# Attention and two expert layers on one core: values product of the float32 tiles turned over, last two experts of the fill on two PSUM banks

## The chip, the cores and the metric

The kernel runs on one core of a Trainium2 chip. The metric is the device time of one execution in microseconds (us). Five engines work side by side, each through its own queue in order: PE (matrix products, with PEld for its weight loads), DVE, ACT, POOL, and SP, which here only issues transfers (DMA).

## The reference, cut to what matters

```
q, k, v: (4, 8, 576, 64)           # batch, heads, tokens, head width
scores = q @ k^T / 8
keep, in each row, the scores >= the 32nd largest; softmax over them
x = attn @ v                        # then laid out as 2304 tokens x 512
h = x @ w_in;  x = (h * cos(h)) @ w_out            # w_in 512x2048, first layer
P = exp(x @ w_gate - max), 8 rounds of row and column scaling   # 2304 x 8
out = sum over e of P[:, e] * (relu(x @ w1[e]) @ w2[e])         # 8 experts, 512x1024x512
```

## The kernel before

A Python planner records every operation with a cost, the buffers that it reads and writes and a priority by engine and class of work, then plays the engines forward and emits the operations in the order in which its own clock would start them. Each engine then runs its queue in that fixed order. An operation may be planned ahead of earlier recorded ones, but never ahead of a recorded one that uses the same buffer: `add` (L120 on) makes a write wait for every operation recorded earlier that reads or writes that buffer.

Nearly all products are made of three float32r products: `mm3` splits both sides into a high and a low part and issues high x high (L372), low x high (L373) and high x low (L374). The first three token tiles (384 tokens) go through plain float32 products instead.

The program in the order in which it is recorded:

- Decode of w_in and w_out (DVE, ACT, POOL), beside it the **first attention**: `attention_tile(0..2)`, three tiles of 128 tokens with 8 heads each. Each head runs `att_tile` with `plain`: scores (L451) to ACT, eight-at-a-time maximum and replace three times on DVE (L459, L464, L465), the masked exponentials with their row sum (L466), the reciprocal (L469), the multiplication of the whole 128x576 tile by it on POOL (L470), five transposes on PE (L475), copies to `at_f` on ACT (L479). Then `attention_tile` itself multiplies by v (L530), which puts a head's 64 output columns on partitions and the tokens on the free side in `ps_t`, and ACT copies this into `x_f` (L534).
- The first layer of those tiles in float32 (`moe1_tile_a` and `moe1_tile_b`, L629 to L661), into `x2fh`, `x2fl`.
- `attention(0, LEAD)`: the rest of batch 0, now with the split products (L447, L448, L501, L503).
- **First block of the fill**: `fill(e, 0, LEAD, two)` for the 8 experts and the first 384 tokens. For each of 8 column groups f of w1 a product into one PSUM bank from a ring (`h_ring`), ReLU and split by ACT and DVE (`gates`, L758, L759), and the product with w2 into `ps_y`.
- `attention(1)`, first layer for 512 tokens (`moe1`, then `keep_parts` into `x2fh`, `x2fl`), `attention(2)`, `attention(3)`.
- **Second block of the fill**: `fill(e, LEAD, 4, ...)` for 8 experts and those 512 tokens. The ring of banks is `two` (`ps_g`, `ps_h`) for e below 6 and `three` (`ps_g`, `ps_s`, `ps_h`) for e = 6 and 7:

```
    two, three = Cycle([ps_g, ps_h]), Cycle([ps_g, ps_s, ps_h])
    ...
    for e in range(NE):
        fill(e, LEAD, 4, two if e < 6 else three)
```

- The first layer of the other 1408 tokens in three parts (`moe1` on the ring `three`), the gating, and then all experts for the last 1408 tokens (`mixed_first`, `plain_first`, `mixed_second`), with which the program ends.

`ps_s` is also where every score product of every attention tile goes (L447, L448, L451), and `ps_t` takes transposes and values products. There are 8 banks in all: `ps_y` (4), `ps_h`, `ps_t`, `ps_s`, `ps_g`.

Of the kernel before, what the change touches and what calls it, by code (L numbers as in the profile page):

```python
# [229 lines left out]
def fused_kernel(tc, kq, vv, w_in, w_out, w_gate, w1, w2, out, B=4):  # L230
# [179 lines left out]
    at_r = ring_of("first", 2, [128, 5, 128], F32, "at_f")  # L410
    xf_r = ring_of("first", 2, [128, 4, 128], F32, "x_f")
# [24 lines left out]
    def att_tile(stats, dests, plain=None):  # L436
# [33 lines left out]
        put("POOL", 724, lambda: G_.tensor_scalar(ex.ap, ex.ap, mc(35), 0.0, op0=ALU.mult, op1=ALU.add), [ex, (m, 35, 36)], [ex])  # L470
        pt = lambda: ps_t.ap.rearrange("p (c t) -> p c t", c=4)
        for c0, c1, p in ((0, 4, 128), (4, 5, 64)):
# [8 lines left out]
            for r0, rn, hd, t0 in dests:  # L481
# [12 lines left out]
                put("DVE", dve_ns(k), lambda hv=hv, sv=sv, lv=lv: V.tensor_tensor(lv(), sv(), hv().bitcast(F32), op=ALU.subtract), [ps_t, hi], [lo])  # L494

# [15 lines left out]
    def attention_tile(t):  # L511

        nonlocal work
        work = "first attention"
        x_f, q = xf_r(), qp_r()
        s0 = t * 128
        dma(lambda: q.ap, lambda: kq[0:H, 0:64, 1, s0 : s0 + 128].rearrange("h d s -> d h s"), 1 << 18, writes=[q], slow=True)
        for pr in range(H // 2):
            k, v = kp_r(), vp_r()
            hs = slice(2 * pr, 2 * pr + 2)  # L520
            dma(lambda k=k, hs=hs: k.ap, lambda hs=hs: kq[hs, 0:64, 0, :].rearrange("h d s -> d h s"), 512 * S, writes=[k], slow=True)
            dma(lambda v=v: v.ap, lambda hs=hs: vv[hs].rearrange("h p c d -> p h c d"), 128 * 2560, writes=[v])
            for j in range(2):
                at_f = at_r()
                att_tile([], [], dict(q=q, k=k, at=at_f, h=2 * pr + j))

                def av(v=v, j=j, at_f=at_f):
                    for c in range(5):
                        p = 64 if c == 4 else 128
                        T_.matmul(ps_t.ap[:64, :128], v.ap[:p, j, c, :], at_f.ap[:p, c, :], start=c == 0, stop=c == 4)  # L530

                put("PE", 1100.0, av, [v, at_f], [ps_t])
                r = slice(64 * j, 64 * j + 64)
                put("ACT", act_ns(128, psum=True), lambda pr=pr, r=r: A_.activation(x_f.ap[r, pr, :], ps_t.ap[:64, :128], AF.Copy), [ps_t], [(x_f, pr, pr + 1)])  # L534
        work = "mlp"
        return x_f
# [477 lines left out]
    for e in range(NE):  # L1014
        fill(e, LEAD, 4, two if e < 6 else three)
# [78 lines left out]
```

## Time and profile before

| | us |
|---|---|
| three runs | 2527.22, 2522.58, 2526.36 (median 2526.36) |
| profiled execution | 2523.42 |
| its span on the core | 2521.6 |
| mean granted TensorE clock | 0.971 of full speed |

The span is the time from the first to the last instruction; the profiled execution's own time is 1.8 us more. Busy time of PE is modelled for pipelined products, so neighbouring matmul rows overlap: the distance of their starts is what a product costs in a row of them. "Rows" of the trace give the start, the duration, engine and line, then output and inputs.

### The profile page before, as it was taken

What the parts mean: (1) busy time and instruction counts of PE and PEld (TensorE: products, weight loads), DVE (VectorE), ACT (ScalarE), POOL (GpSimd) and SP (SyncE); (2) the same over time, 40 slices, a digit from 0 to 9 for tenths busy, and PEclk for the clock granted to TensorE, in tenths of its full rate; (3) what the DMA queues carried; (4) which work ended last, traced back from release to release, by engine and by line L of the source; (5) the groups of instructions that cost most, each with busy time, mean ns of one, the idle gap of its engine ahead of it and who ended that gap; (6) DMA issues with size and microseconds to landing.
All of it is one profiled execution on the core that took longest, in us unless ns stands there. A gap on an engine that the chain in (4) does not pass through costs nothing.

```text
span 2521.6 us, 33547 instructions
## 1 busy us (share of the span) xinstructions
PE 2389.5 (95%) x11089; PEld 1919.8 (76%) x11089; DVE 1981.5 (79%) x3651; ACT 1272.9 (50%) x2438; POOL 1265.6 (50%) x1328
## 2 busy tenths in 40 slices
PE   6888999999889999997799999999999999999999
PEld 3444688888667877776588788788888888888887
DVE  8997599999989999999927778776666665666655
ACT  6785576666578656565346767422222222232221
POOL 6886587777676656565340113533333434444330
PEclk9779999999899999998799999999999999999999
DMA  8765654444322433332043333112222221111101
GB/s 265 228 211 185 201 155 150 137 139 131 99 91 78 120 116 117 109 117 77 26 132 114 106 108 115 48 55 79 71 72 84 84 72 34 34 34 46 38 21 46
DMA packets 159501, 261.37 MB, mean 104 GB/s; under 512 B 15008, under 2 KB 60656, under 8 KB 159328
## 3 DMA queue, kind: packets, MB, share of 16 engines
q1 hardware_dynamic: 159328, 259.24, 33.9%
q8 instruction: 87, 1.43, 0.2%
q14 instruction: 86, 0.70, 0.1%
HBM read 227.31 MB, written 31.87 MB: 103 GB/s over the span
## 4 chain that ended last, share of the span: by engine, by line
PE 56%; DVE 22%; POOL 4%; issue 3%; ACT 3%; DMA 1%; POOLq 0%; ACTq 0%; DVEq 0%
PE y L372 9%; PE y L373 9%; PE y L374 9%; DVE wk L464 6%; DVE m L465 5%; DVE ex L466 3%; PE g L374 2%; PE g L373 2%; PE g L372 2%; DVE atl L494 2%; DVE m L459 2%; POOL wlo L347 1%; PE y L383 1%; PE y L384 1%; PE y L387 1%
## 5 line engine op out<-in xcount | busy, mean ns | idle before, releaser
L347 POOL TENSOR_TENSOR wlo<-raw,whi 128x512 fp32r<-128x512 f32 x336 | 452.7, 1351 | 203.0 <-ACT whi L345 131.9
L465 DVE MAX8 m<-wk 128x8 f32<-128x576 f32 x432 | 318.0, 748 | 1.8
L953 DVE SCALAR_TENSOR_TENSOR acc<-y,P,acc 128x512 f32<-128x512 f32 x308 | 229.2, 748 | 103.4 <-PE y L374 103.0
L345 ACT ACTIVATE whi<-raw 128x512 fp32r<-128x512 f32 x416 | 258.9, 626 | 97.3 <-PE y L374 34.0
L464 DVE MATCH_REPLACE8 wk<-m,wk 128x576 f32<-128x576 f32 x288 | 213.6, 742 | 1.2
L475 PE MATMUL t<-ident,ex 128*128 128x128 f32 (+1 forms) x720 | 143.3, 301 | 55.8 <-DVE atl L494 20.6
L475 PEld LDWEIGHTS t<-ident,ex 128*128 128x128 f32 (+1 forms) x720 | 89.5, 145 | 122.3 <-DVE atl L494 32.4
L372 PE MATMUL y<-whi,gh 128*128 128x512 f32 x448 | 181.6, 405 | 0.0
L372 PE MATMUL y<-gh,xh 128*128 128x512 f32 x450 | 176.0, 391 | 1.0 <-DVE acc L949 1.0
L374 PE MATMUL y<-whi,gl 128*128 128x512 f32 x448 | 176.5, 394 | 0.0
L373 PE MATMUL y<-wlo,gh 128*128 128x512 f32 x448 | 175.9, 393 | 0.0
L373 PE MATMUL y<-gl,xh 128*128 128x512 f32 x450 | 175.5, 390 | 0.0
L374 PE MATMUL y<-gh,xl 128*128 128x512 f32 x450 | 175.4, 390 | 0.0
L457 ACT ACTIVATE sc<-s 128x288 f32<-128x288 f32 x288 | 117.0, 406 | 97.4 <-DVE ex L466 55.6
L466 DVE SCALAR_TENSOR_TENSOR ex<-sc,m,ex 128x576 f32<-128x576 f32 x144 | 149.7, 1039 | 3.6 <-ACT ex L461 1.8
L493 ACT ACTIVATE ath<-t 64x128 fp32r<-64x128 f32 (+3 forms) x272 | 104.5, 396 | 58.9 <-PE t L475 52.2
L470 POOL TENSOR_SCALAR ex<-ex,m 128x576 f32<-128x576 f32 x144 | 111.4, 774 | 38.1 <-DVE m L469 36.0
L461 ACT ACTIVATE ex<-sc,m 128x576 f32<-128x576 f32 x144 | 111.2, 772 | 32.1 <-POOL m L460 31.0
L459 DVE MAX8 m<-sc 128x8 f32<-128x576 f32 x144 | 106.9, 743 | 8.7 <-ACT sc L457 8.6
L464 DVE MATCH_REPLACE8 wk<-m,sc 128x576 f32<-128x576 f32 x144 | 106.7, 741 | 0.0
L468 POOL TENSOR_SCALAR m<-m 128x1 f32<-128x1 f32 x144 | 29.2, 202 | 146.5 <-DVE ex L466 141.3
L372 PEld LDWEIGHTS y<-gh,xh 128*128 128x128 f32 x450 | 84.5, 188 | 19.6 <-DVE acc L949 1.8
(384 smaller groups left out, 7150.5 us busy)
## 6 DMA issues: line engine op xcount, KB each, us to landing
raw<-in_w_dram SPq DMA_DIRECT2D x384, 256.0 KB, 2.6
kq<-in_kq_dram SPq DMA_DIRECT2D x32, 576.0 KB, 4.1
raw<-win_d SPq DMA_DIRECT2D x64, 256.0 KB, 3.0
raw<-wout_d SPq DMA_DIRECT2D x64, 256.0 KB, 2.7
y_d<-st SPq DMA_DIRECT2D x56, 256.0 KB, 3.0
raw<-y_d SPq DMA_DIRECT2D x56, 256.0 KB, 2.6
wp<-win_d SPq DMA_DIRECT2D x24, 512.0 KB, 5.0
wp<-wout_d SPq DMA_DIRECT2D x24, 512.0 KB, 4.4
```

The costliest lines, as they stand in the source:

```text
L345: put("ACT", act_ns(n), lambda: A_.activation(hv(), rv(), AF.Copy), [rb], [hb])
L347: put(e, c, lambda: f.tensor_tensor(lv(), rv(), hv().bitcast(F32), op=ALU.subtract), [rb, hb], [lb])
L372: T_.matmul(o(), ah(), bh(), start=start, stop=False)
L373: T_.matmul(o(), ah(), bl(), start=False, stop=False)
L374: T_.matmul(o(), al(), bh(), start=False, stop=stop)
L457: put("ACT", act_ns(288, psum=True), lambda c=c: A_.activation(sc.ap[:, c], o(), AF.Copy), [ps_s], [(sc, c.start, c.stop)])
L459: put("DVE", 669, lambda: V.max(mc(0, 8), sc.ap), [sc], [(m, 0, 8)])
L464: put("DVE", 669, lambda r=r, src=src: V.match_replace(wk.ap, mc(8 * r, 8), src.ap, LOWEST), [src, (m, 8 * r, 8 * r + 8)], [wk])
L465: put("DVE", 669, lambda r=r: V.max(mc(8 * r + 8, 8), wk.ap), [wk], [(m, 8 * r + 8, 8 * r + 16)])
L466: put("DVE", 729, lambda: V.scalar_tensor_tensor(ex.ap, sc.ap, mc(31), ex.ap, op0=ALU.is_ge, op1=ALU.mult, accum_out=mc(33)), [sc, ex, (m, ...
L475: T_.transpose(pt()[:p, c - c0, :], ex.ap[:, c * 128 : c * 128 + p], ident.ap)
L953: put("DVE", 663, lambda y=y, av=av, pcol=pcol: V.scalar_tensor_tensor(av(), y.ap, pcol(), av(), op0=ALU.mult, op1=ALU.add), [y, P, a], [a])
```

## The change

Two things are changed.

1. In the float32 tiles the POOL multiplication by the reciprocal of the row sum goes. The values product takes the attention weights `at_f` as the stationary side and v as the moving one, so the tokens stand on output partitions and a head fills 64 columns of `ps_g`. ACT evicts these 64 columns into a new tile `x_t` (128 tokens x 512) and multiplies by the reciprocal, one number a partition, in the same instruction. After the eighth head four transposes into `ps_t` and one ACT copy make `x_f` as it was.
2. Experts 6 and 7 of the second block of the fill use the ring of two banks as well.

```
+    xt_r = ring_of("first", 2, [128, 512], F32, "x_t")
...
-        put("POOL", 724, lambda: G_.tensor_scalar(ex.ap, ex.ap, mc(35), 0.0, op0=ALU.mult, op1=ALU.add), [ex, (m, 35, 36)], [ex])
+        if not plain:
+            put("POOL", 724, lambda: G_.tensor_scalar(ex.ap, ex.ap, mc(35), 0.0, op0=ALU.mult, op1=ALU.add), [ex, (m, 35, 36)], [ex])
...
-                        T_.matmul(ps_t.ap[:64, :128], v.ap[:p, j, c, :], at_f.ap[:p, c, :], start=c == 0, stop=c == 4)
-
-                put("PE", 1100.0, av, [v, at_f], [ps_t])
-                r = slice(64 * j, 64 * j + 64)
-                put("ACT", act_ns(128, psum=True), lambda pr=pr, r=r: A_.activation(x_f.ap[r, pr, :], ps_t.ap[:64, :128], AF.Copy), [ps_t], [(x_f, pr, pr + 1)])
+                        T_.matmul(ps_g.ap[:, d], at_f.ap[:p, c, :], v.ap[:p, j, c, :], start=c == 0, stop=c == 4)
+
+                put("PE", 1100.0, av, [v, at_f], [(ps_g, h, h + 1)])
+                put("ACT", act_ns(64, psum=True, ap=True), lambda d=d, rv=rv: A_.activation(x_t.ap[:, d], ps_g.ap[:, d], AF.Copy, scale=rv()), [(ps_g, h, h + 1), rb], [(x_t, h, h + 1)])
+
+        def tr():
+            for c in range(4):
+                T_.transpose(ps_t.ap[:, c * 128 : c * 128 + 128], x_t.ap[:, c * 128 : c * 128 + 128], ident.ap)
+
+        put("PE", 436.0, tr, [x_t, ident], [ps_t])
+        put("ACT", act_ns(512, psum=True), lambda: A_.activation(x_f.ap, ps_t.ap.rearrange("p (c t) -> p c t", c=4), AF.Copy), [ps_t], [(x_f, c, c + 1) for c in range(4)])
...
-        fill(e, LEAD, 4, two if e < 6 else three)
+        fill(e, LEAD, 4, two)
```

The planner makes a new order out of it on every engine. (In the changed kernel the lines after the first edit count a few more: scores L448 and L449, transposes L477, values products L504 and L506.) Three places of PE's queue:

PE before, late in `attention(3)`: the last score products (into `s`), transposes (into `t`), and then the first fill product of the group that takes the bank `s`. There is no fill product in the 82 rows ahead of it.

```order
L448 MATMUL s_107<-kl1_1425,qt1_1380 128x288
L475 MATMUL t_226<-ident_82,ex2_223 64x128
L475 MATMUL t_226<-ident_82,ex0_137 128x128 x4
L447 MATMUL s_107<-kh0_1383,qt0_1372 128x288
L448 MATMUL s_107<-kl0_1388,qt0_1372 128x288
L447 MATMUL s_107<-kh1_1400,qt1_1380 128x288
L448 MATMUL s_107<-kl1_1425,qt1_1380 128x288
L475 MATMUL t_226<-ident_82,ex0_137 64x128
L372 MATMUL s_107<-x2fh_1460,whi2_1681 128x512
L373 MATMUL s_107<-x2fl_1463,whi2_1681 128x512
```

All score products of the kernel stand ahead of the first fill product into `s`.

PE in the change, the same stretch of `attention(3)`: score products for the same 64-token tile (`qt`) and fill products into `h` and `y`.

```order
L374 MATMUL y3_1327<-whi1_1620,gl7_2134 128x512
L448 MATMUL s_107<-kh1_1358,qs1_1374 128x288
L449 MATMUL s_107<-kl1_1366,qs1_1374 128x288
L372 MATMUL h_735<-x2fh_1467,whi2_1625 128x512
L373 MATMUL h_735<-x2fl_1469,whi2_1625 128x512
L374 MATMUL h_735<-x2fh_1467,wlo2_1644 128x512
L372 MATMUL h_735<-x2fh_1467,whi2_1625 128x512
L373 MATMUL h_735<-x2fl_1469,whi2_1625 128x512
L374 MATMUL h_735<-x2fh_1467,wlo2_1644 128x512
L477 MATMUL t_195<-ident_82,ex0_137 128x128 x4
L448 MATMUL s_107<-kh0_1295,qt0_1278 128x288
L449 MATMUL s_107<-kl0_1306,qt0_1278 128x288
```

The fill of the last two experts now runs between the scores. By the last attention product of the kernel PE has issued 477 of the 512 high x high products of the fill's first halves in the order before, and 511 in the change.

PE in the change, the end of attention: the last values product (`vs`), the last fill product into `g` and the products into `y` that follow it. The first layer's next part begins 28 rows behind the last values product; before, it begins 226 rows behind it.

```order
L506 MATMUL t_195<-atl1_1887,vs1_1391 128x320
L504 MATMUL t_195<-ath1_1874,vs1_1391 128x320
L372 MATMUL g_229<-x2fh_1467,whi0_1614 128x512
L373 MATMUL g_229<-x2fl_1469,whi0_1614 128x512
L374 MATMUL g_229<-x2fh_1467,wlo0_1622 128x512
L372 MATMUL y0_654<-whi1_1620,gh6_2052 128x512
```

## Rows read from the trace of the kernel before

**Rows 1.** The page's slices: PE, DVE and granted clock, tenths in 40 slices.
```profile
PE   6888999999889999997799999999999999999999
...
DVE  8997599999989999999927778776666665666655
...
PEclk9779999999899999998799999999999999999999
```

**Rows 2.** Windows: us, busy (count) of PE, PEld, DVE, ACT, POOL, clock, DMA.
```profile
882.00:1008.00 126.00, 123.24 (x617) 99.26 (x617) 123.46 (x267) 76.21 (x165) 75.79 (x97) 1.00 0.38 116
...
1450.00:2521.00 1071.00, 1058.73 (x4886) 896.82 (x4884) 706.34 (x1051) 350.79 (x609) 395.51 (x334) 1.00 0.20 61
```

**Rows 3.** Windows of 20 us around the end of attention, same columns.
```profile
1100.00:1120.00 20.00, 19.64 (x97) 15.11 (x96) 19.84 (x42) 13.68 (x30) 13.03 (x18) 1.00 0.54 173
...
1160.00:1180.00 20.00, 16.87 (x86) 13.01 (x85) 19.59 (x43) 13.75 (x30) 14.39 (x19) 0.98 0.35 99
1180.00:1200.00 20.00, 8.91 (x28) 5.71 (x27) 19.81 (x46) 7.48 (x16) 3.34 (x9) 0.50 0.00 0
1200.00:1220.00 20.00, 9.92 (x41) 7.52 (x41) 19.81 (x47) 7.78 (x19) 4.97 (x11) 0.67 0.04 9
1220.00:1240.00 20.00, 15.03 (x56) 11.34 (x54) 19.74 (x47) 6.65 (x15) 2.37 (x7) 0.57 0.02 5
1240.00:1260.00 20.00, 18.41 (x85) 14.04 (x85) 18.53 (x42) 9.12 (x18) 11.50 (x15) 1.00 0.24 68
```

**Rows 4.** PE's timeline: fill's last and next products, next part's first.
```profile
1173.89 0.39 PE L373 MATMUL g<-x2fl,whi 128*128 128x512 f32 x1
1174.13 0.40 PE L374 MATMUL g<-x2fh,wlo 128*128 128x512 f32 x1
...
1231.76 0.44 PE L448 MATMUL s<-kl,qt 128*128 128x288 f32 x1
...
1232.70 0.79 PE L372 MATMUL s<-x2fh,whi 128*128 128x512 f32 x1
...
1322.17 0.39 PE L372 MATMUL s<-xh,whi 128*128 128x512 f32 x1
```

**Rows 5.** DVE's timeline: a gate's low part, the last masked exponentials.
```profile
1241.57 0.68 DVE L759 SCALAR_TENSOR_TENSOR gl<-s,gh 128x512 fp32r<-128x512 f32 x1
...
1256.67 0.82 DVE L466 SCALAR_TENSOR_TENSOR ex<-sc,m,ex 128x576 f32<-128x576 f32 x1
```

**Rows 6.** Timelines of DVE, POOL, ACT and PE, first attention's end.
```profile
225.38 0.92 DVE L466 SCALAR_TENSOR_TENSOR ex<-sc,m,ex 128x576 f32<-128x576 f32 x1
...
231.61 0.75 POOL L470 TENSOR_SCALAR ex<-ex,m 128x576 f32<-128x576 f32 x1
...
241.01 0.27 ACT L534 ACTIVATE x_f<-t 64x128 f32<-64x128 f32 x1 [2.08 <-PE t L530]
...
242.73 1.88 PE L629 MATMUL y<-wp,x_f 128*128 128x512 f32 x4
...
287.07 0.39 PE L372 MATMUL g<-x2fh,whi 128*128 128x384 f32 x1
```

**Rows 7.** Groups by shape, 0 to 290 us: count, busy us, mean ns, idle before.
```profile
L466 DVE SCALAR_TENSOR_TENSOR ex<-sc,m,ex 128x576 f32<-128x576 f32 x26 | 31.4, 1206 | 0.3
...
L470 POOL TENSOR_SCALAR ex<-ex,m 128x576 f32<-128x576 f32 x26 | 21.3, 818 | 7.9 <-DVE m L469 7.7
...
L479 ACT ACTIVATE at_f<-t 128x512 f32<-128x512 f32 x24 | 14.2, 590 | 7.6 <-PE t L475 7.6
...
L534 ACT ACTIVATE x_f<-t 64x128 f32<-64x128 f32 x24 | 6.4, 268 | 14.4 <-PE t L530 14.0
```

**Rows 8.** Groups of PE, 0 to 290 us, same columns.
```profile
L530 PE MATMUL t<-at_f,vp 128*64 128x128 f32 (+1 forms) x240 | 43.2, 328 | 7.2 <-ACT at_f L479 7.2
...
L475 PE MATMUL t<-ident,ex 128*128 128x128 f32 (+1 forms) x129 | 31.2, 354 | 15.9 <-ACT at_f L479 6.8 <-POOL ex L470 4.5 <-ACT x_f L534 2.2
```

**Rows 9.** Groups by shape of DVE, 1180 to 1240 us, same columns.
```profile
L466 DVE SCALAR_TENSOR_TENSOR ex<-sc,m,ex 128x576 f32<-128x576 f32 x9 | 7.3, 812 | 0.2
```

More of the change, by code (lines that the diff above doesn't have):

```diff
@@ L494, in att_tile @@
                 put("DVE", dve_ns(k), lambda hv=hv, sv=sv, lv=lv: V.tensor_tensor(lv(), sv(), hv().bitcast(F32), op=ALU.subtract), [ps_t, hi], [lo])
+        return (m, 35, 36), lambda: mc(35)
     def att_out(hd, x32, j, n):
@@ L514, in attention_tile @@
         work = "first attention"
-        x_f, q = xf_r(), qp_r()
+        x_f, x_t, q = xf_r(), xt_r(), qp_r()
         s0 = t * 128
@@ L521, in attention_tile, with av @@
             dma(lambda k=k, hs=hs: k.ap, lambda hs=hs: kq[hs, 0:64, 0, :].rearrange("h d s -> d h s"), 512 * S, writes=[k], slow=True)
-            dma(lambda v=v: v.ap, lambda hs=hs: vv[hs].rearrange("h p c d -> p h c d"), 128 * 2560, writes=[v])
+            dma(lambda v=v, hs=hs: v.ap, lambda hs=hs: vv[hs].rearrange("h p c d -> p h c d"), 128 * 2560, writes=[v])
             for j in range(2):
-                at_f = at_r()
-                att_tile([], [], dict(q=q, k=k, at=at_f, h=2 * pr + j))
-                def av(v=v, j=j, at_f=at_f):
+                at_f, h = at_r(), 2 * pr + j
+                rb, rv = att_tile([], [], dict(q=q, k=k, at=at_f, h=h))
+                d = slice(h * 64, h * 64 + 64)
+                def av(v=v, j=j, at_f=at_f, d=d):
                     for c in range(5):
                         p = 64 if c == 4 else 128
-                        T_.matmul(ps_t.ap[:64, :128], v.ap[:p, j, c, :], at_f.ap[:p, c, :], start=c == 0, stop=c == 4)
-                put("PE", 1100.0, av, [v, at_f], [ps_t])
-                r = slice(64 * j, 64 * j + 64)
-                put("ACT", act_ns(128, psum=True), lambda pr=pr, r=r: A_.activation(x_f.ap[r, pr, :], ps_t.ap[:64, :128], AF.Copy), [ps_t], [(x_f, pr, pr + 1)])
+                        T_.matmul(ps_g.ap[:, d], at_f.ap[:p, c, :], v.ap[:p, j, c, :], start=c == 0, stop=c == 4)
[6 more added lines that the diff above has]
+        put("ACT", act_ns(512, psum=True), lambda: A_.activation(x_f.ap, ps_t.ap.rearrange("p (c t) -> p c t", c=4), AF.Copy), [ps_t], [(x_f, c, c + 1) for c in range(4)])
         work = "mlp"
```

## Prediction

> **What bounds the kernel now.** I read the page's slices first. Each slice is 63 us. DVE shows eights and nines up to the twentieth, but for the fourth and fifth, and drops after; PE shows nines from the fifth slice on, except for eights in the eleventh and twelfth and two sevens in the nineteenth and twentieth, 1135 to 1260 us [rows 1]. So there are two halves. While attention runs (to about 1260 us) DVE and PE are both full: 123.5 and 123.2 of 126 us in one window. After 1450 us only PE is: 1059 of 1071 us, with DVE at 706 [rows 2]. What changes the end is therefore time in which PE does not get ahead; the reader should look for stretches where PE is idle or at the lower clock and ask what it waits for.
>
> The largest such stretch is the end of attention. In the windows of 20 us PE falls from 19.6 us busy to 8.9, 9.9 and 15.0, with the granted clock at 0.50, 0.67 and 0.57, so mostly at 1.2 GHz, while DVE stays at 19.7 to 19.8 [rows 3]. PE's timeline says what is missing: no fill product between 1174.1 and 1232.7 us. The next one writes `ps_s` and starts just after the last score product of the kernel (1231.8) [rows 4]. That is the rule of the planner: fill products recorded after all attention may not take `ps_s` before all score products are through. Experts 6 and 7 use that bank; their second halves accumulate in order of f, so the group that waits for it holds the rest. From 1232.7 PE then works off the two experts, alone after attention ends, until the next part starts at 1322.2 [rows 4]. That start is my mark: behind it PE is the bound in both kernels and the queues hold the same work.
>
> **The ring of two banks, what it gives.** Lost time of PE in a window is its idle time plus busy time times (1 - clock), if work at 1.2 GHz takes twice as long (an estimate). From 1160 to 1260 us: 3.5 + 15.5 + 13.4 + 11.4 + 1.6 = 45.4 us; five windows of full running lose 5 x 0.36 = 1.8 us [rows 3]. **-44 us**, if PE has fill work at hand all the time. It has: the order of the change puts the products of experts 6 and 7 between the scores, and 511 of 512 of the counted products are issued by the last attention product, where it was 477. The same mix of attention and fill ran before with PE at 19.64 and DVE at 19.84 of 20 us [rows 3], so the mix itself has a row.
>
> **What is given back.** In the order PE stands further behind attention than before when it gets there: at the 600th of the 720 transposes of attention probabilities it has issued 2348 fill products against 2396. 48 products by 0.23 to 0.24 us from start to start [rows 4] are **+11 us**, which come after that point instead of ahead of it.
>
> DVE gets 8 gates (low parts) ahead of its last masked exponentials that it did later before: 8 x 0.6 to 0.68 us = 5 us [rows 5]. On DVE's own path the end comes at 1256.7 + 5 us and the shift of the start (below, 5 us): 1267; from there the last tile needs transposes, evictions and its values product among the last fill products, some 70 rows of PE, 17 us by 0.23 us each. That is 1284 us, ahead of PE's own path (1322 - 44 + 11 + 5 = 1294), so these gates cost nothing as long as PE is the later one; that cover is 10 us.
>
> **The float32 tiles.** Removed: 24 POOL multiplications of 0.82 us [rows 7]. They sit on the way from the row sum to the transposes. In the middle of the first attention this is hidden, since DVE is full. At its end it is not: the last masked exponentials start at 225.4, the last POOL multiplication runs only at 231.6, behind work of the next attention in POOL's queue, and the last copy into `x_f` is at 241.0 [rows 6], 15 us in all. In the change this chain is five transposes (31.2 / 26 = 1.2 us a head), two copies (0.6 and 0.3), the values product (43.2 / 24 = 1.8 us), the scaled copy (0.3), four transposes (1.0) and a copy (0.6 us) [rows 7, 8]: 5.8 us and some eight hand-overs; I take 7 us, so 8 us sooner.
>
> The values product: 240 records, two a product, 43.2 us in all [rows 8]. With 64 moving columns for 128 and 128 stationary for 64 the trace has no such form. Its bounds are half the time (-21 us of PE) and the longer of the weight loads showing (0.35 us, the transposes' record of 128 columns [rows 8], +5 us). All of it lies beside DVE's full queue; at the end of the chain one head counts, -0.9 to +0.2 us. I take 0. The scaled eviction of 128x64 stands between the 0.27 us of the old copy and the 0.59 us of a copy of 512 columns [rows 7]; nearest is 0.27, and only the last head's shows. Added are 12 transposes and 3 copies of 512 columns, of which one set per tile is in the chain above.
>
> Against that stands the order. Behind the last float32 values product PE now has 50 float32 products of the first layer ahead of the fill, where it had 44: six by 0.86 us (four records, two products, in 1.88 us, less the overlap with the next [rows 6]), +5 us. With 5 us that DVE gains earlier (next part) the fill, which began at 287.1 us [rows 6], begins near 279. But DVE then has 20 rows of attention less behind it (310 rows ahead of its first gate, 330 before). An instruction of DVE takes 0.46 us on the mean of a window [rows 2] and 0.81 us for a pass over 576 columns [rows 9], which most of these are: 9 to 16 us, I take 13. Attention is thus late by 13 - 8 = **+5 us**. Bounds: -5 (the chain gains as above and DVE makes the rows good in a gap) and +13 (no gain at the start).
>
> **A rule weighed.** The masked exponentials, with two inputs from SBUF, take 1.21 us in the first 290 us, where POOL decodes, and 0.81 us from 1180 to 1240, where POOL is nearly idle [rows 7, 9]. So POOL's work stretches DVE's: 26 x 0.39 = 10 us in this group alone. Removing 20 us of POOL's work should return a part of that; I take 5 us, half of this group's, counted above. The Trainium skill, "SBUF — State Buffer", section "Who interferes with whom", says that the two share a port pair as an exclusive lock held for a whole instruction, so that the later one fully blocks; by it the removed work could return up to its whole 20 us, and the sum would be 15 us lower. The rows show stretching of the size of a part, not of all of it; the full size is a rival below.
>
> **Sum.** -44 + 11 + 5 = -28 us on the profiled execution's 2523.4 us (span 2521.6): 2495.4. The profiled execution is 2.9 us under the median of the runs, and within their 2522.6 to 2527.2; I forecast about half of that more: **2497 us** as the median.
>
> **Rivals.**
> - *More comes back.* POOL's removed work returns nearly in full to DVE's stage, 15 us more: 2482. For: the gap between 1.21 and 0.81 us [rows 7, 9]. Against: most of POOL's work there is decode, which stays. Chance 0.17, times 2473 to 2487.
> - *Less comes back.* The start costs its full 13 us (8 more than taken), and DVE's eight gates (5 us) come into the path: 2497 + 13 = 2510. For: DVE is at 19.8 of 20 us throughout [rows 3]; it has nothing to give. Chance 0.18, times 2507 to 2521.
> - *Nothing comes back.* At the join, the next part's weights are split on DVE, where before it was idle for some 60 us ahead of it; now these splits queue behind the last attention tiles. If PE waits there for 28 us, the gain is gone. Against: DVE has about 15 instructions of 0.3 to 0.7 us there in the order, under 10 us. Chance 0.06, near 2522.
> - *Slower.* Fill products now stand ahead of scores in PE's queue when DVE has no slack. DVE does 9 masked exponentials in 60 us [rows 9], so about 12 tiles fall in the stretch from 1174 to 1257. If every tile's scores waited for a whole pass of one f, 24 products or 5.6 us, with DVE idle meanwhile, that costs 12 x 5.6 = 67 us: 2497 + 67 = 2564. It decides from 28 / 12 = 2.3 us a tile. Against: in the same mix DVE lost 0.16 us in 20 [rows 3]. Chance 0.04.
> - That the change doesn't do what it says is excluded for the banks by the order: no fill product into `s` is left.
>
> **How the numbers follow.** My forecast (2487 to 2507) has 0.55, the rivals 0.17, 0.18, 0.06 and 0.04. Bounds: start -5 to +13, give-back 0 to 11, lost time 36 to 46. The range 2479 to 2515 takes the forecast, half of each neighbour and a little more, about 0.8. What a measurement can tell from no change is about 0.2%, 5 us. Faster by more: 0.55 + 0.17 + 0.18 = 0.90; within: 0.06; slower: 0.04.
>
> **What would show it.** Right: in the last 80 us of attention PE at 19 us and more of 20 with clock 1.00, fill products into `g` and `h` all along, and the first product of the next part within 1284 to 1304 us instead of 1322. The start: last copy into `x_f` 8 to 12 us sooner, first fill product near 279. Wrong: if PE stays busy there but that mark hardly moves, work was displaced rather than gained; if DVE falls under 19 of 20 us there, the slower rival is at work; if the mark moves and the end doesn't, the later half took it back.

## The result, and the profile after

The changed kernel takes **2491.4 us** (median of 4 runs, 2489.5 to 2491.6) against 2525.9 of the kernel before (4 runs): ratio 0.9864, 95% interval 0.9847 to 0.9881, so 34.5 us faster. The forecast was 2497 with a range of 2479 to 2515. The profiled execution took 2491.60 us, its span is 2489.8 (before 2521.6).

The slices of the page, PE, DVE and granted clock, to be laid beside [rows 1] (a slice is 62 us now):

```profile
PE   6879999999788999999999999999999999999999
...
DVE  8995599999999999999967777776666666666655
...
PEclk9969999999889999999999999999999999999999
```

The two sevens of PE in the nineteenth and twentieth slices are gone. What is left of PE's losses lies in the first three slices and in the eleventh to thirteenth, and DVE's dip in the fourth and fifth slice, a seven and a five before, is two fives now. It will matter.

The end of attention in windows, same columns as [rows 3]:

```profile
1160.00:1180.00 20.00, 20.00 (x103) 16.58 (x103) 19.59 (x45) 14.40 (x32) 14.52 (x19) 1.00 0.36 117
1180.00:1200.00 20.00, 19.87 (x99) 16.10 (x98) 19.81 (x43) 11.14 (x23) 11.40 (x15) 1.00 0.28 84
1200.00:1220.00 20.00, 20.00 (x105) 16.50 (x104) 19.67 (x46) 12.37 (x27) 11.27 (x15) 1.00 0.26 75
1220.00:1240.00 20.00, 18.77 (x93) 14.69 (x93) 19.77 (x40) 11.78 (x25) 8.84 (x12) 1.00 0.41 125
1240.00:1260.00 20.00, 20.00 (x101) 16.50 (x100) 19.81 (x44) 10.55 (x20) 10.76 (x14) 1.00 0.30 84
```

PE is full at 2.4 GHz (clock 1.00) where it had 8.9 to 15.0 of 20 us at 0.50 to 0.67; DVE is as full as before. The mark, the first product of the next part, and DVE's last masked exponentials (timelines of PE and DVE):

```profile
1266.57 1.82 DVE L467 SCALAR_TENSOR_TENSOR ex<-sc,m,ex 128x576 f32<-128x576 f32 x1
```

```profile
1286.20 0.39 PE L372 MATMUL g<-xh,whi 128*128 128x512 f32 x1
```

The mark is 36.0 us sooner than the 1322.17 of [rows 4], and the last masked exponentials 9.9 us later than in [rows 5]. Of the 36 us the span keeps 31.8. The other 4.2 are lost again in one place: in the 200 us around the end of the first layer (1464 to 1664, with 1500 to 1700 as its counterpart before) the window between 1524 and 1544 has 16.43 us of PE at a clock of 0.84, where its counterpart had 18.28 at 0.91, and by the same sum of idle and slow time the whole stretch loses 14.7 against 10.5 us. PE's one wait in that window is 3.6 us for a high part that ACT makes (`gh`); its counterpart before has one of 1.5 us, for another. The window (PE, clock, DMA) and the wait (in all, times, longest):

```profile
1524.00:1544.00 20.00, 16.43 (x81) 0.84 0.36 96
```

```profile
PE y L383 <- ACT gh L345: 3.6, 1, 3.6
```

The start, from the timelines of DVE, ACT, PE and DVE again (compare [rows 6]): last masked exponentials of the first attention, last copy into `x_f`, first fill product, and the first masked exponentials of the other attention (the 25th of the kernel).

```profile
218.18 0.82 DVE L467 SCALAR_TENSOR_TENSOR ex<-sc,m,ex 128x576 f32<-128x576 f32 x1
...
285.35 1.38 DVE L467 SCALAR_TENSOR_TENSOR ex<-sc,m,ex 128x576 f32<-128x576 f32 x1
```

```profile
225.41 0.60 ACT L544 ACTIVATE x_f<-t 128x512 f32<-128x512 f32 x1 [1.18 <-PE t L541]
```

```profile
277.45 0.39 PE L372 MATMUL g<-x2fh,whi 128*128 128x384 f32 x1
```

All of the first attention's end is sooner: 7.2 us at the exponentials, 15.6 at `x_f`, 9.6 at the first fill product. But the 25th masked exponentials, which ran at 240.78 us in the kernel before, start 44.6 us later, and between 219 and 278 DVE mostly stands still: its longest waits there are 8.8 (up to 228.3), 8.1, 10.3 and 16.5 us, all for the first layer of the float32 tiles.

```profile
237.10 1.23 DVE L600 TENSOR_TENSOR rr<-rr,hs 128x1024 f32<-128x1024 f32 x1 [8.11 <-POOL rr L599]
...
259.14 0.69 DVE L679 TENSOR_TENSOR x2fl<-y,x2fh 128x512 fp32r<-128x512 f32 x1 [10.29 <-ACT x2fh L678]
276.29 0.69 DVE L679 TENSOR_TENSOR x2fl<-y,x2fh 128x512 fp32r<-128x512 f32 x1 [16.45 <-ACT x2fh L678]
```

The debt shows where DVE is the bound. The 72nd masked exponentials, the last that the first layer's 512 tokens wait for, before and after:

```profile
656.74 0.80 DVE L466 SCALAR_TENSOR_TENSOR ex<-sc,m,ex 128x576 f32<-128x576 f32 x1
```

```profile
666.24 0.81 DVE L467 SCALAR_TENSOR_TENSOR ex<-sc,m,ex 128x576 f32<-128x576 f32 x1
```

PE, which has run out of fill at 644 us in both kernels, waits for them. Windows of 644 to 805 us, before and after (all engines, columns as in [rows 2]):

```profile
644.00:805.00 161.00, 134.52 (x607) 105.15 (x606) 148.93 (x270) 115.09 (x200) 108.80 (x108) 0.92 0.29 86
```

```profile
644.00:805.00 161.00, 127.09 (x572) 97.88 (x571) 156.21 (x290) 107.92 (x191) 103.18 (x111) 0.89 0.28 82
```

Lost time of PE there (161 less busy times clock) rises from 37.2 to 47.9 us. So the change has two sides: a gain at the end of attention and a loss in the middle. The first runs take them apart.

### The profile page after: what moved, and what is told of

It is laid out like the page before. It is cut to its first block, busy times and chain, and to the rows that moved or that the text cites. A ratio compares the mean times of both kernels' runs of the same rounds, so it can differ in the third digit from the quotient of the medians.

```text
span 2489.8 us, 33497 instructions
## 1 busy us (share of the span) xinstructions
PE 2372.2 (95%) x11101; PEld 1922.6 (77%) x11101; DVE 1985.1 (80%) x3651; ACT 1270.5 (51%) x2437; POOL 1250.5 (50%) x1304
## 4 chain that ended last, share of the span: by engine, by line
PE 49%; DVE 5%; ACT 1%; POOL 1%; issue 1%; DMA 0%; SPq 0%; POOLq 0%; ACTq 0%; DVEq 0%
PE y L372 8%; PE y L374 8%; PE y L373 8%; PE g L374 2%; PE g L373 2%; PE g L372 2%; PE y L383 1%; PE y L384 1%; PE y L387 1%; PE y L896 1%; PE y L895 1%; PE s L895 1%; PE y L897 1%; PE s L897 1%; PE h L897 1%; PE h L895 1%
## 5 line engine op out<-in xcount | busy, mean ns | idle before, releaser
L347 POOL TENSOR_TENSOR wlo<-raw,whi 128x512 fp32r<-128x512 f32 x336 | 458.8, 1370 | 223.4 <-ACT whi L345 132.9
L477 PE MATMUL t<-ident,ex 128*128 128x128 f32 (+1 forms) x720 | 140.6, 296 | 46.1 <-DVE ex L467 13.9
L477 PEld LDWEIGHTS t<-ident,ex 128*128 128x128 f32 (+1 forms) x720 | 87.3, 143 | 112.4 <-DVE ex L467 20.9
L467 DVE SCALAR_TENSOR_TENSOR ex<-sc,m,ex 128x576 f32<-128x576 f32 x144 | 158.7, 1102 | 1.3
L472 POOL TENSOR_SCALAR ex<-ex,m 128x576 f32<-128x576 f32 x120 | 90.3, 752 | 31.4 <-DVE m L470 28.9
L372 PE MATMUL y<-gh,gh 128*128 128x512 f32 x254 | 99.1, 390 | 0.0
```

What stands on the lines that cost most here:

```text
L347: put(e, c, lambda: f.tensor_tensor(lv(), rv(), hv().bitcast(F32), op=ALU.subtract), [rb, hb], [lb])
L372: T_.matmul(o(), ah(), bh(), start=start, stop=False)
L467: put("DVE", 729, lambda: V.scalar_tensor_tensor(ex.ap, sc.ap, mc(31), ex.ap, op0=ALU.is_ge, op1=ALU.mult, accum_out=mc(33)), [sc, ex, (m, ...
L477: T_.transpose(pt()[:p, c - c0, :], ex.ap[:, c * 128 : c * 128 + p], ident.ap)
```

## The experiments

Each kernel ran beside the kernel before on the same chip. "After" in the diffs is the changed kernel. The kernel before took 2523.1 to 2525.9 us (medians) beside them, so the difference of two rows that did not run together is good to 2 or 3 us; the first four rows ran together, and so did mul_kept, mul_twice, att_first and banks_att_first.

| run | median, us | ratio to before, 95% interval |
|---|---|---|
| banks_only | 2482.5 | 0.9835 (0.9821 to 0.9848) |
| float_only | 2524.8 | 1.0006 (0.9997 to 1.0014) |
| three_last | 2484.5 | 0.9844 (0.9831 to 0.9858) |
| three_from_5 | 2570.7 | 1.0186 (1.0172 to 1.0200) |
| mul_kept | 2506.7 | 0.9937 (0.9924 to 0.9949) |
| mul_twice | 2499.9 | 0.9908 (0.9895 to 0.9922) |
| att_first | 2457.0 | 0.9740 (0.9727 to 0.9753) |
| banks_att_first | 2476.3 | 0.9818 (0.9804 to 0.9831) |
| att_first_three | 2467.4 | 0.9777 (0.9764 to 0.9791) |
| att_first_mul | 2475.0 | 0.9805 (0.9792 to 0.9819) |
| att_first_act | 2463.5 | 0.9762 (0.9749 to 0.9775) |
| one_tile_ahead | 2477.1 | 0.9813 (0.9800 to 0.9826) |

### The two parts alone

**banks_only**, the kernel before with

```
-        fill(e, LEAD, 4, two if e < 6 else three)
+        fill(e, LEAD, 4, two)
```

> The kernel before with the second edit alone (experts 6 and 7 on two banks, float32 tiles as they were). Theory: the lost PE time of the end of attention (about 45 us between 1160 and 1260) comes back and nothing is paid at the start, since PE has issued the same 412 of 512 high x high products at the 600th transpose of attention probabilities as before: first product of the next part near 1277 (1322 - 45), some 4 us of it given back behind that mark as in the changed kernel, 2485 us (2480 to 2491), thus below the changed kernel's 2491. Rival: the float32 edit gives the kernel 8 us at the start, so without it the time is 8 us and more above the changed kernel, 2497 to 2503. A third: the two parts do nothing for one another and the bank edit gives only the 28 us of the forecast's sum, 2497 to 2500.

Measured 2482.5 us, near the theory's 2485, and 9 us below the changed kernel by the medians (6 by what each gains on the kernel before beside it; the two intervals just touch). The mark, and the last values product of attention (PE's timeline):

```profile
1273.31 0.39 PE L372 MATMUL g<-xh,whi 128*128 128x512 f32 x1
...
1285.49 0.31 PE L501 MATMUL t<-ath,vs 128*128 128x320 f32 x1
```

The mark is 48.9 us sooner than before. But here 5 transposes and 18 values products of attention still stand behind it, which take PE some 4 us (before and in the changed kernel none does), so about 45 us compare. The bank edit is thus worth some 41 us of time by itself, and the float32 edit took 6 to 9 of them away.

**float_only**, after with

```
-        fill(e, LEAD, 4, two)
+        fill(e, LEAD, 4, two if e < 6 else three)
```

> The changed kernel with the ring of three banks for experts 6 and 7 again, so the float32 edit alone. Theory: PE begins the second block of the fill late, as in the changed kernel (820 against 804 us), but that lateness only shortens the stretch in which PE stands still for the bank of the scores, so the next part begins where it did (1322, -3 to +4) and the time is that of the kernel before, 2526 (2521 to 2531). Rival 1, parts that add: it costs the 16 us of the forecast (11 + 5), 2537 to 2543. Rival 2: it is worth the 8 us by which its first attention ends sooner, 2515 to 2520.

Measured 2524.8, no difference from before. So the parts do not add: the same edit costs 6 to 9 us with the banks and nothing without. The second block of the fill starts 15.5 us late (819.0 against 803.5), but PE has a hole to absorb it: it stands waiting for the bank later, and the first fill product into `s` comes at 1234.87, behind the last score at 1233.93, as in [rows 4].

### Is it the bank, or how much work it bars?

**three_from_5** makes the wait longer, the kernel before with

```
-        fill(e, LEAD, 4, two if e < 6 else three)
+        fill(e, LEAD, 4, two if e < 5 else three)
```

> The kernel before with three experts (5, 6, 7) on the ring of three: the wait made longer. Theory: the first fill product into the scores' bank still has to wait for the last score product, and 33 more of the counted high x high products stand behind it (428 ahead of the last score, 460 before); each stands for six products of 0.23 us, so 33 x 6 x 0.23 = 46 us more of PE's work is pushed behind the end of attention: 2568 (2555 to 2575), with the last fill product before the gap near 1110 us. Rival: the bank is not what PE waits for in that stretch (PE has nothing to do because DVE is the bound), then the time stays 2526 within 5.

Measured 2570.7, so 47.6 us slower for a computed 46. The last fill product ahead of the gap, the last score and the first fill product behind it (PE's timeline), and PE in the gap (windows, columns as in [rows 2]):

```profile
1116.40 0.39 PE L374 MATMUL g<-x2fh,wlo 128*128 128x512 f32 x1
...
1229.28 0.44 PE L448 MATMUL s<-kl,qt 128*128 128x288 f32 x1
1230.22 0.79 PE L372 MATMUL s<-x2fh,whi 128*128 128x512 f32 x1 [0.50 <-ACT sc L457]
```

```profile
1120.00:1160.00 40.00, 22.34 (x73) 16.61 (x74) 39.62 (x94) 15.38 (x35) 9.78 (x22) 0.52 0.07 19
```

For 113 us attention runs alone: DVE is full, PE half busy at half speed. That is the stretch that [rows 3] showed, doubled. DVE does not get ahead by it: the last score is at 1229.3, before at 1231.8.

**three_last** bars only expert 7, the kernel before with

```
-        fill(e, LEAD, 4, two if e < 6 else three)
+        fill(e, LEAD, 4, two if e < 7 else three)
```

> The kernel before with only expert 6 moved to two banks; expert 7 keeps the ring of three, and so the wait for the last score product. Theory: what costs is the amount of fill that is barred from the time of attention, not the bank itself. In the order PE has issued 493 of 512 high x high products of the fill ahead of the first that writes the scores' bank (460 before), so hardly any stretch without fill is left ahead of the last score: within 4 us of the kernel with both experts on two banks. Rival: each expert on the third bank costs its half, so the time lies in the middle between the kernel before and the one with both on two banks, about 2505.

Measured 2484.5, 2 us from both experts on two banks, and not the middle. Its mark is 9.3 us later than that of banks_only (1282.62), but some 4 of these are the attention that banks_only still has behind its mark, and 5 come back behind the mark, where this kernel lacks the wait of 3.6 us (more on it in the section on why the prediction was right). So half of the edit gives nearly all of the gain: what costs is the fill work that is left when the ring first asks for the barred bank, counted against the attention that is still to run.

### Which part of the float32 edit costs?

**mul_kept**, after with the POOL multiplication kept on the float32 tiles:

```
-        if not plain:
+        if True:
             put("POOL", 724, lambda: G_.tensor_scalar(ex.ap, ex.ap, mc(35), ...
...
-                put("ACT", act_ns(64, psum=True, ap=True), ... A_.activation(x_t.ap[:, d], ps_g.ap[:, d], AF.Copy, scale=rv()), ...
+                put("ACT", act_ns(64, psum=True), ... A_.activation(x_t.ap[:, d], ps_g.ap[:, d], AF.Copy), ...
```

> The changed kernel, but the float32 tiles keep the POOL multiplication (values product still turned over, its eviction without the scale). PE's order at the start stays that of the changed kernel (120 transposes of attention probabilities ahead of the first fill product). Theory: the multiplication matters only at the end of the first attention, where it is in the chain: last copy into x_f some 4 to 6 us later than 225.4, and what the 20 us of POOL's work take from DVE beside it is small, so 2494 (2489 to 2499). Rival, the rule weighed in the prediction at its full size: DVE and POOL exclude one another, the 20 us come back whole: 2506 to 2512. A third: it costs nothing and the order of the start was what cost: 2491 within 2.

Measured 2506.7, 15 us above the changed kernel: my theory said 3, the first rival 15 to 21. The last masked exponentials, the last multiplication and the last copy into `x_f` (timelines of DVE, POOL and ACT):

```profile
221.81 1.96 DVE L467 SCALAR_TENSOR_TENSOR ex<-sc,m,ex 128x576 f32<-128x576 f32 x1
```

```profile
225.28 1.78 POOL L472 TENSOR_SCALAR ex<-ex,m 128x576 f32<-128x576 f32 x1
```

```profile
234.97 0.60 ACT L544 ACTIVATE x_f<-t 128x512 f32<-128x512 f32 x1
```

`x_f` is 9.6 us later, 3.6 of them at the masked exponentials and 6.0 in the chain behind them; the first fill product is 13.4 later (290.87), the mark 12.1 (1298.34). Masked exponentials of DVE up to 228 us, this kernel and the changed one (groups by shape, columns as in [rows 7]):

```profile
L467 DVE SCALAR_TENSOR_TENSOR ex<-sc,m,ex 128x576 f32<-128x576 f32 x24 | 30.4, 1268 | 0.1
```

```profile
L467 DVE SCALAR_TENSOR_TENSOR ex<-sc,m,ex 128x576 f32<-128x576 f32 x24 | 25.9, 1080 | 0.1
```

Only 4.5 us are stretched exponentials. PE's waits up to 228 us show what else is held up (in all, times, longest), in this kernel, in the changed one and in the kernel before:

```profile
PE s L452 <- ACT sc L458: 25.8, 20, 7.9
PE t L477 <- POOL ex L472: 12.8, 9, 4.2
```

```profile
PE s L452 <- ACT sc L458: 16.4, 15, 2.7
PE t L477 <- DVE ex L467: 13.9, 8, 2.9
```

```profile
PE s L451 <- ACT sc L457: 10.8, 14, 1.6
...
PE t L475 <- POOL ex L470: 2.2, 3, 0.9
```

Ahead of the transposes PE waits 12.8 us for the multiplication, where it waits 13.9 for DVE without it; but for the eviction of scores it waits 9 us more, at one time 7.9 us. In the kernel before, with the same 24 multiplications in another order, these are 2.2 and 10.8 us. So the multiplication has no fixed price. And the 15 us are not shown to be its own: the planner makes another order for this kernel too (on PE the two part at the 7th operation, though 120 transposes stand ahead of the first fill product in both), and no run holds the order.

**mul_twice**, mul_kept with one more pass on the plain path:

```
+        if plain:
+            put("POOL", 724, lambda: G_.tensor_scalar(ex.ap, ex.ap, 1.0, 0.0, op0=ALU.mult, op1=ALU.add), [ex], [ex])
```

> As the run before, with a second POOL pass over the 128x576 tile (times 1) behind the multiplication: 24 more instructions of 0.8 us, some 20 us of POOL. The order made of it differs in one place: it puts one tile of the other attention ahead of the first fill product again, as in the kernel before (125 transposes, not 120). Theory: that tile fills a gap of DVE of some 8 us at the start, which outweighs the longer chain of the first attention (one more POOL pass, 1 to 5 us): not slower than the kernel with one multiplication, 2485 to 2494. Rival 1: POOL's passes are what costs: 4 to 10 us above that kernel, by the rule at full size 20 us above. Rival 2: neither order nor pass matters: equal within 2.

Measured 2499.9: above the 2485 to 2494 that I gave, but 7 us faster than with one pass, against both rivals. One more pass cannot help; another order can. This pointed at the order, but with two things changed at once, and the orders differ in more than the one tile that I named: on PE they part at the 13th operation.

**one_tile_ahead** changes the order alone. In the changed kernel

```
-                put("PE", 1100.0, av, [v, at_f], [(ps_g, h, h + 1)])
+                put("PE", 1000.0, av, [v, at_f], [(ps_g, h, h + 1)])
```

> The changed kernel with every instruction as it is, but the planner counts 1000 for a float32 values product where it counted 1100. The only effect is another order: score products of two tiles of the other attention stand among the first layer's products, and the transposes of one of them (125 by then) ahead of the first fill product, as in the kernel before. Theory: the changed kernel's 9 us against the bank edit alone are this order: with the 25th masked exponentials back at about 240 us (285 in the changed kernel) and the 26th near 275, DVE's attention is 7 to 10 us sooner, and the time falls to 2482 (2477 to 2486). Rival: the order of the start is not what costs, but the float32 products turned over and their transposes: 2491 within 3.

Measured 2477.1, 14 us below the changed kernel (12 by what each gains on the kernel before beside it). The 25th masked exponentials (DVE's timeline; the 26th start at 269.16):

```profile
232.85 0.82 DVE L467 SCALAR_TENSOR_TENSOR ex<-sc,m,ex 128x576 f32<-128x576 f32 x1
```

The 72nd come at 654.4 (666.24 in the changed kernel), the mark at 1272.9. Every instruction is the same and only their order differs, by a guess of one cost that is 9% less. So the order alone is worth more than the whole loss against the bank edit: in this one the float32 edit *gains* some 5 us on the bank edit alone (2477.1 against 2482.5, with intervals that overlap). It is not shown that the one tile does it all. The two orders part at PE's 27th operation, and some things move all along. But 11.8 of the 13.3 us at the mark are there at the 72nd exponentials, and what is seen ahead of them is this tile: its masked exponentials come 52.5 us sooner.

### The gap of DVE as the lever

**att_first**, after with the priorities of PE for attention and for the first layer of the float32 tiles exchanged:

```
-    "PE": (0, 1, 9, 2, 3),
+    "PE": (0, 2, 9, 1, 3),
```

> The changed kernel, with the planner's priorities on PE for the other attention and the first layer of the float32 tiles exchanged (attention ahead of first layer). In the order nine tiles of attention (165 - 120 = 45 transposes) now stand ahead of the first fill product. Theory: the changed kernel loses its 9 us against the bank edit alone because DVE idles some 45 us between 228 and 278 us and the attention of batch 1, for which PE waits between 644 and 820 (48 us of lost PE time there), ends late; with that gap filled the attention ends 25 to 45 us sooner, the first fill product comes 20 to 40 us later (300 to 315), and the time falls to 2470 (2455 to 2485). Rival: PE is the bound from the start, what is put ahead only pushes the fill back and nothing is recovered: 2491 to 2510.

Measured **2457.0**, 34 us below the changed kernel (32 by what each gains on the kernel before beside it) and 67 below the kernel before: the fastest here. Windows of this kernel around the gap and in the middle, behind them the changed kernel's row of the gap (columns as in [rows 2]):

```profile
228.00:290.00 62.00, 56.93 (x247) 32.46 (x246) 59.94 (x127) 45.16 (x94) 39.51 (x53) 1.00 0.74 242
644.00:805.00 161.00, 144.22 (x691) 115.11 (x690) 151.16 (x284) 121.36 (x216) 123.71 (x119) 0.98 0.35 102
```

```profile
228.00:290.00 62.00, 58.49 (x206) 32.74 (x205) 18.83 (x34) 25.10 (x47) 18.37 (x18) 0.97 0.64 207
```

DVE has 59.9 of 62 us where it had 18.8, PE is as busy as before (56.9 and 58.5). The first fill product comes 27 us later (304.68), and still the mark is 35 us sooner (1251.25), because PE's lost time from 644 to 805 falls from 47.9 to 19.7 us.

**banks_att_first**, the same exchange in banks_only.

> The bank edit alone (float32 tiles as before) with the same exchange of priorities on PE. Theory: the same gap of DVE is there (the 26th masked exponentials started at 276 us, the 24th at 225), 10 us smaller by the one tile that runs in it; so 8 to 20 us below the bank edit alone: 2467 (2455 to 2476). Rival: as above, nothing recovered: 2482 to 2500.

Measured 2476.3: 6 us less, just outside what was expected (2455 to 2476). The gap of DVE is filled as well as in att_first (58.6 of 62 us busy from 228 to 290, where banks_only has 21.1), but PE's lost time from 644 to 805 falls only from 37.4 us in banks_only to 25.7 (window of this kernel):

```profile
644.00:805.00 161.00, 139.53 (x663) 110.60 (x662) 149.99 (x280) 121.30 (x210) 122.51 (x119) 0.97 0.33 101
```

The second block of the fill even starts 5.4 us later than in banks_only (811.3 against 805.9), where in att_first it starts 25.3 us sooner than in the changed kernel. Why was not traced. With the same exchange of priorities the float32 edit, with the order that comes with it, is therefore worth 19 us. The next run takes out one part of it.

**att_first_mul**, the same exchange in mul_kept.

> The kernel with attention ahead of the first layer on PE, with the POOL multiplication of the float32 tiles kept (values product turned over, eviction without the scale). In the changed kernel it cost 15 us to keep it: its chain at the end of the first attention ended 9.6 us later, and only 4.5 us of its cost were longer masked exponentials (30.4 against 25.9 us for 24). Theory: with DVE busy through that chain, only the stretched exponentials and the later start of the first layer's products count: 4 to 10 us, 2464 (2461 to 2467). Rival: the multiplication takes 15 us and more wherever it stands, 2472 to 2480. A third: nothing, 2457 within 2.

Measured 2475.0: 18 us above att_first, so the rival held. My theory took the multiplication as a matter of the chain at the end of the first attention, hidden once DVE has other work. It is not hidden: up to 228 us PE waits 10.9 us for it and 23.3 for the eviction of scores (11.9 in att_first), the last copy into `x_f` is at 239.03 against 227.33 us, the first fill product at 321.64 against 304.68 and the 25th masked exponentials at 245.05 against 225.08. The orders of the two kernels are not quite alike, so that not all of the 18 need be the multiplication.

**att_first_three**, att_first with the ring of three for experts 6 and 7 again.

> The kernel with attention ahead of the first layer on PE, but experts 6 and 7 of the second block on the ring of three again, so the bank edit taken back. In the order 461 of the 512 high x high products are issued at the first fill product into the scores' bank, and 464 were issued at the last score product of the kernel with two banks: only 3 x 6 products of 0.23 us, 4 us, are barred. Theory: what costs is the amount of fill barred from the time of attention; here attention ends sooner and the fill later, so the bank edit is worth hardly anything, 2460 (2455 to 2466). Rival: the third bank itself costs, whatever the order: 20 to 45 us, 2477 to 2502.

Measured 2467.4, 10 us above att_first, where the bank edit was 41 (banks_only). It fell with the amount that is barred, as the theory says; its size was above my range. The mark is even 16.0 us later (1267.22), and 4.6 come back behind it, where this kernel lacks the wait of 3.6 us. I counted the barred products (4 us). But there is no fill product from 1164.7 to 1177.1 us, and lost time of PE from 1150 to 1210 is 3.0 + 9.5 + 1.4 = 14 us by these windows of PE (busy, clock, DMA), where att_first loses 0.1:

```profile
1150.00:1170.00 20.00, 17.30 (x93) 0.98 0.37 121
1170.00:1190.00 20.00, 12.37 (x51) 0.85 0.05 17
1190.00:1210.00 20.00, 18.57 (x91) 1.00 0.24 70
```

What stands still is PE for as long as attention still needs at DVE's pace, which is more than the products behind the wait would take.

**att_first_act**, a try for more, att_first with

```
-    "ACT": (0, 0.5, 1, 2, 1.5),
+    "ACT": (0, 0.5, 1, 0.4, 1.5),
```

> A try for more: the kernel with attention ahead of the first layer on PE, and attention's evictions ahead of all else but the first attention in ACT's order as well. In the trace of that kernel DVE is idle 10 us of the 161 from 644 to 805, and 5 of the 355 after it: attention can end some 10 us sooner at the most, and the fill's gates on ACT come later. Theory: DVE is the bound until attention ends and has nothing more to give, so no change: 2457 (2452 to 2462). Rival: ACT is where PE's lost 20 us between 644 and 805 come from: 2440 to 2450.

Measured 2463.5, 6.5 us slower than att_first, just above my range: DVE had nothing more to give. That the fill's evictions came late for it is likely and was not looked into.

## Why the prediction was right, point by point

- **The cause at the end of attention** (the planner's rule on `ps_s`) was right: banks_only, three_last and three_from_5 came within 3 us of the numbers worked out from it. The term, -44 us, measured 48.9 at the mark of banks_only, some 45 without the attention that stands behind that mark, and 41 in the time.
- **What is lost behind the mark** is missing from the prediction, which said that the queues hold the same work there. They do, but in another order. The three parts of the first layer that follow the fill take their banks from the same ring of three as experts 6 and 7 did, and the ring counts on: without those experts' 16 turns the next part begins at `g` instead of `s` [rows 4]. Eight kernels here begin it at `g` with no attention left behind the mark, and run 1203.5 to 1206.0 us from the mark to the end of the span; three_from_5, with the float32 tiles and the ring of before but 24 turns, is one of them (1204.9). The four that begin at `s` or `h` (before, float_only, three_last, att_first_three) run 1198.8 to 1199.5. The wait of 3.6 us (3.8 in one_tile_ahead) stands in the trace of each kernel here that begins at `g`, and in none of those four. So the bank edit most likely pays some 4 us for moving a ring that later work shares; it is not shown by itself, since no run moves the ring alone.
- **"What is given back" and the start, +11 and +5**, together 16: 12.9 us at the two marks, 9 with the attention behind that of banks_only counted, 6 to 9 in the time (after against banks_only). The kinds were right, the size was nearly twice what came. "Attention is thus late by +5" was 9.5 at the 72nd exponentials.
- **The step that failed** is "DVE then has 20 rows of attention less behind it ... 9 to 16 us, I take 13", which I set off against the 8 us of the chain, and then treated as a small net cost that comes with the edit. The row counts were read rightly, but not what they meant: it is one whole tile of attention that the planner happened to leave out, in an order that costs 12 to 14 us against another order of the same instructions (one_tile_ahead). The gap of DVE behind it, 43 of 62 us in the changed kernel, was on the page before in nearly its full size (the seven and the five in [rows 1]; 41 us in this window of the kernel before), and I did not ask what it would be worth to fill it: 32 to 34 us in the changed kernel, 6 with the bank edit alone.

```profile
228.00:290.00 62.00, 56.77 (x202) 29.88 (x203) 21.41 (x40) 24.98 (x46) 18.11 (x23) 0.96 0.60 192
```

- **The chain of the float32 tiles.** 7 us from the last masked exponentials to `x_f` was forecast, 7.2 measured; 8 to 12 us sooner was forecast for `x_f`, 15.6 measured, of which 7.2 came from DVE (I took 5). From `x_f` to the first fill product it takes 52.0 us, before 46.1: the six more float32 products, +5 forecast, are 6.0.
- **The values product** was taken as no gain, with bounds of -21 and +5 us: 43.2 us before [rows 8], 47.2 now for the same 240 products, with half the moving columns and twice the stationary ones. The scaled eviction of 64 columns is 303 ns, the old copy was 268 [rows 7]. Groups of PE up to 1290 us, and of ACT up to 290:

```profile
L534 PE MATMUL g<-vp,at_f 128*128 128x64 f32 (+1 forms) x240 | 47.2, 353 | 1.4 <-ACT at_f L481 1.4
```

```profile
L537 ACT ACTIVATE x_t<-g,m 128x64 f32<-128x64 f32 x24 | 7.3, 303 | 6.8 <-PE g L534 6.7
```

- **The eight gates** on DVE cost nothing at the end: attention's last values product ended 6 us ahead of the mark, where the forecast had a cover of 10.
- **The rule weighed.** I read 1.21 against 0.81 us as stretching "of the size of a part". The single instructions say otherwise: of the first 24 masked exponentials in the changed kernel 16 take less than 0.9 us and 6 take 1.67 us or more. Two of them, with the POOL instruction beside each (timelines of DVE and POOL):

```profile
45.97 0.81 DVE L467 SCALAR_TENSOR_TENSOR ex<-sc,m,ex 128x576 f32<-128x576 f32 x1
...
52.68 1.67 DVE L467 SCALAR_TENSOR_TENSOR ex<-sc,m,ex 128x576 f32<-128x576 f32 x1
```

```profile
46.12 1.78 POOL L332 TENSOR_TENSOR d_low<-d_low,d_sgn 128x512 f32<-128x512 f32 x1 [0.36 <-DVE d_sgn L331]
...
52.47 1.27 POOL L333 TENSOR_TENSOR d_low<-d_mag,d_low 128x512 f32<-128x512 f32 x1
```

  Where DVE starts first (by 0.15 us) it takes its 0.81, and POOL 1.78, where the same instruction otherwise takes 1.27. Where POOL starts first (by 0.21) it takes 1.27, and DVE 1.67. The Trainium skill, "SBUF — State Buffer", section "Who interferes with whom", says that whoever issues first holds the shared pair and the other blocks; by these rows the trace agrees in the main, and a mean hid it: the one that waits ends 0.61 us behind the other's end, a little less than its own 0.81. The rival that carried the rule's full size ("more comes back", 15 us) had the size that mul_kept measured, 15 us, but only 4.5 of these are DVE's wait for POOL; the rest is in the chain behind it or in the order. The changed kernel did not come out at that rival's 2482; the same instructions in another order did (2477.1).

- **The rivals that forecast less or a loss** did not show: DVE stays at 19.6 to 19.8 of 20 us to the end of attention, which speaks against fill products starving it, and the mark moved, which speaks against a wait for DVE at the join.

In sum the forecast was 5.6 us high: 1 us more came from the end of attention (45 for 44), 7 less was given back (9 for 16), and 4 were lost behind the mark, which makes some 4 us of the span; the rest is what I had added for the median over the profiled execution, which the runs of the changed kernel don't show (2491.4 and 2491.6). That two of these errors point opposite ways is luck; that the largest term came out is not.

What stays open: mul_kept is 24 us above banks_only, with the multiplication in both. The order may be 12 to 14 of them, if it costs there what it costs without the multiplication (one_tile_ahead). The rest may be the turned-over product with its transposes and copies, or PE's longer waits with the multiplication in this order (25.8 against 10.8 us for the eviction of scores); no run has either by itself.

## What to carry to other kernels

When a planner writes the order, an edit changes two things, its instructions and the order; run the edit in more than one order (here one cost in the planner made another) before its price is believed. Where one engine bounds a stage, the idle time of that engine *ahead* of the stage is the first thing to look for, though its length is not its price: some 40 us of DVE idle behind the first attention were worth 32 to 34 us in the changed kernel and 6 with the bank edit alone. A ring of banks that later work shares moves with an edit, and that can cost later (here, most likely, some 4 us). And a wait on a shared bank costs the time that its owner still needs when the waiter first asks: moving one of two experts off the bank gave nearly all, three on it doubled the loss.

## What the runs showed of the hardware that was not expected

DVE's masked exponentials and POOL's passes do not share: either takes its own time, or waits out most of what is left of the other's (0.81 or 1.67 us and more for DVE, 1.27 or 1.78 for POOL's 128x512 subtraction). Of the first 24 masked exponentials of the changed kernel 8 start behind a POOL pass that is still running, and each ends 0.61 to 0.62 us behind that pass's end, whatever was left of it; the 11 that start ahead of a subtraction of L332 (by 0.16 or 0.17 us) take their 0.81, and each of these subtractions ends 1.13 or 1.14 us behind them. The other passes of DVE over the same 576 columns take the same time with and without the multiplications beside them: maxima 744 against 746 ns, replacements 738 in both (groups of DVE up to 228 us, the changed kernel and mul_kept).

```profile
L466 DVE MAX8 m<-wk 128x8 f32<-128x576 f32 x72 | 52.5, 744 | 0.0
L465 DVE MATCH_REPLACE8 wk<-m,wk 128x576 f32<-128x576 f32 x48 | 35.4, 738 | 0.0
```

```profile
L466 DVE MAX8 m<-wk 128x8 f32<-128x576 f32 x72 | 53.0, 746 | 0.1
L465 DVE MATCH_REPLACE8 wk<-m,wk 128x576 f32<-128x576 f32 x48 | 35.4, 738 | 0.0
```
